# Five loads of raw input weights move from SyncE's queue to ScalarE's, in a channel attention with a SiLU feed-forward layer

## Chip, cores and metric

The kernel runs on one core of one Trainium2 chip. The metric is the device time of one execution in microseconds (us), and the median of several executions is compared.

## What is computed

The reference, cut to what matters: a channel attention over two batches, whose output is the input of a feed-forward layer with SiLU.

```python
def _attn_ref(q, k, v, tau):                       # q, k, v: 2 x 6016 x 256
    qn = q / (np.linalg.norm(q, axis=1, keepdims=True) + 1e-06)
    kn = k / (np.linalg.norm(k, axis=1, keepdims=True) + 1e-06)
    s = kn.transpose(0, 2, 1) @ qn / tau           # 2 x 256 x 256
    a = np.exp(s - s.max(-1, keepdims=True))
    a /= a.sum(-1, keepdims=True) + 1e-09
    return (v @ a).astype(np.float32)

def _moe_ref(x, w_in, w_out):                      # x: 12032 x 256
    h = x @ w_in                                   # 256 x 2048
    g = h * (1.0 / (1.0 + np.exp(-h)))
    return (g @ w_out).astype(np.float32)
```

w_in and w_out come to the chip as 64-bit words, a raw form that the kernel decodes to float.

## The kernel before

The attention matrix of a batch is 256 x 256. So it is computed first and multiplied into w_in; after that the tokens, 1024 at a time, go through a feed-forward layer with the mixed weights. That second part takes some 900 us and is PE's alone. The change lies in the first stage, the first 50 us, which works on batch 0:

- **q and k.** `load_qk` (line 230) brings rows of k and q side by side. The 47 rows j of batch 0 come as four small tiles `g` of one row and then as tiles `kq_t` of two rows (512 KB; the 22nd and last has one row). Seven buffers of pool `st` hold them, so a load waits until the tile seven places back has been read. PE multiplies each tile into the scores `sc` (line 301).
- **Norms.** `attention` squares each tile on ACT (line 296, into `sq`, a tag with two buffers that the squares of v_t use too) and adds the squares up on DVE (line 298, into `acc`, which lies in the space of `wo`). At the end DVE adds the two halves of `acc` (line 292) and the square of the last, half tile. Then PE sums over the partitions: `tot` (line 318), ACT takes the root, DVE the reciprocals `rn` (line 357), and so on to the attention matrix.
- **Raw weights.** `load_wi(j)` (line 1176) loads one of eight blocks of w_in, 512 KB in rows of 2 KB, through `land` (line 172), which issues the DMA. Blocks 0 to 4 go to tiles `raw`, blocks 5 to 7 to the tile `held`. DVE takes the largest value of each (`raw_amax`, line 213, into `raw_max`). Block 0 is decoded early: a CAST on ACT (line 203) and a shift with an OR on DVE (line 205), into `t`.
- **v.** `load_v` brings 1024 tokens of v; `scale_v` squares them on ACT (line 522), takes differences on DVE (lines 585 and 642), and scales and splits them on ACT and DVE (lines 164 and 165).
- **tau** is loaded, spread over the partitions by a matmul `tau_ps` and inverted on DVE.

Each engine works through its instructions in the order in which they stand in the program. That order comes from a scheduling layer, which goes by priorities (the first stage has priority 0, the maxima of the raw blocks a later one) and by its own estimate of when things are ready; only from line 1316 on is the order of PE and DVE written by hand, and later that of ACT. DMAs share eight completion semaphores in turn, so an issue also waits for the DMA eight places back. Issues from SP and from ACT go to two queues. `follow(load, ...)` holds the issues of a load behind the last instruction of SP so far.

The loop of the first stage (line 1234) goes over all tiles, the four small ones first: the score steps of a tile, then `load_qk` for the tile seven places on, and at g = 6, 8, 10, 12 and 14, which are the `kq_t` tiles 3, 5, 7, 9 and 11, a `load_wi` (line 1242).

## Time and profile before

| | us |
|---|---|
| median of three executions | 1007.92 (1007.48 to 1007.94) |
| the profiled execution | 1006.87 |
| its span in the profile | 1005.10 |
| PE busy in the span | 998.5 (99%) |
| DVE, ACT busy | 847.7, 769.5 |
| software queue of GpSimd, SP's queue: moved | 67.98 MB, 68.84 MB |

The span leaves out 1.8 us of the execution around it. PE's clock is granted in full in all forty slices of the page, and its matmuls follow each other nearly without a gap from the first microseconds to the end. The DMA engines are busy for 90% and more of the first tenth of the span, and for a third to a half of the rest. Matmuls of float32 show as two records each: a `kq_t` tile of two rows has eight records on PE.

### The profile page before, as it was taken

Reading aid. Unit: us, or ns where it says so; the run is one execution under the profiler, and the core shown is the slowest. Engines: PE = TensorE matmul, PEld = TensorE weight load, DVE = VectorE, ACT = ScalarE, POOL = GpSimd, SP = SyncE. Lnnn points to the kernel's source line nnn. Section 1 sums busy time; section 2 is a strip of 40 time slices with the busy share of each in tenths; the row PEclk is TensorE's granted clock in tenths of the full one; section 3 lists DMA queues with packets and bytes.
Section 4 is the critical chain, followed back from the end, with each engine's and each line's share of the span. In section 5 each row is a group of like instructions: output and inputs, shape, how many; then the busy total and the mean of one; then the engine's idle time right before and its main releaser. Section 6 shows DMA issues by size and latency. Waiting matters only on the chain.

```text
span 1005.1 us, 20958 instructions
## 1 busy us (share of the span) xinstructions
PE 998.5 (99%) x8554; PEld 869.1 (86%) x8554; DVE 847.7 (84%) x1334; ACT 769.5 (77%) x1081; POOL 199.5 (20%) x283
## 2 busy tenths in 40 slices
PE   9999999999999999999999999999999999999998
PEld 8877555788888888888999988888888888889998
DVE  6997678888888888899889998888888888888776
ACT  6686798788888888878878777677677677677674
POOL 1011000122222222222222212212212212212231
PEclk9999999999999999999999999999999999999999
DMA  9996200546547547526435335335435335335343
GB/s 368 397 397 219 84 1 1 185 103 193 152 135 201 148 129 201 142 72 166 97 74 133 92 91 153 93 95 142 102 95 145 98 95 150 87 96 127 82 99 87
DMA packets 62053, 138.81 MB, mean 138 GB/s; under 512 B 6659, under 2 KB 20915, under 8 KB 61955
## 3 DMA queue, kind: packets, MB, share of 16 engines
q0 software_dynamic: 30672, 67.98, 29.1%
q1 hardware_dynamic: 30850, 68.84, 19.5%
q8 instruction: 67, 1.10, 0.4%
q10 hardware_dynamic: 432, 0.64, 0.2%
q14 instruction: 32, 0.25, 0.1%
HBM read 57.67 MB, written 12.32 MB: 70 GB/s over the span
## 4 chain that ended last, share of the span: by engine, by line
PE 87%; DVE 5%; DMA 4%; ACT 2%; issue 1%; SPq 0%; DVEq 0%; ACTq 0%
PE o L939 38%; PE x L805 21%; PE y L805 10%; PE z L805 5%; PE o L707 4%; DMA kq_t<-in_kq 4%; PE sc L301 3%; PE x L734 2%; PE w L454 2%; DVE g L812 1%; PE y L734 1%; DVE hl L825 1%; ACT hl L822 1%; DVE t L1035 0%; DVE sb L997 0%
## 5 line engine op out<-in xcount | busy, mean ns | idle before, releaser
L805 PEld LDWEIGHTS <-wall 128*128 128x128 f16 x3696 | 360.0, 98 | 37.4 <-issue 1.1
L805 PE MATMUL x<-m,wall 128*128 128x256 f16 (+1 forms) x2112 | 282.9, 270 | 0.5 <-DVE g L812 0.2
L939 PE MATMUL o<-hl,wo 128*128 128x256 f16 (+1 forms) x2136 | 274.1, 270 | 0.0
L825 DVE SCALAR_TENSOR_TENSOR hl<-g,sg,hl 128x1024 f16<-128x1024 f32 (+1 forms) x176 | 221.1, 1257 | 53.4 <-ACT hl L822 52.8
L939 PEld LDWEIGHTS <-wo 128*128 128x128 f16 x2484 | 242.2, 98 | 23.0
L815 ACT ACTIVATE g<-g,alpha 128x512 f32<-128x512 f32 (+3 forms) x176 | 161.5, 921 | 83.0 <-DVE g L812 81.8
L822 ACT ACTIVATE hl<-g,sg 128x1024 f16<-128x1024 f32 (+1 forms) x176 | 198.0, 1126 | 0.0
L1042 POOL DMA_DIRECT2D sums<-hl x109 | 97.3, 892 | 359.0 <-DMA sums<-hl 123.5
L805 PE MATMUL y<-m,wall 128*128 128x256 f16 (+1 forms) x1056 | 141.7, 270 | 0.1
L846 ACT COPY c<-x 128x512 f32<-128x512 f32 (+1 forms) x88 | 50.7, 576 | 74.5 <-PE x L805 74.5
L939 PE MATMUL o<-t,ws_hi 128*128 128x256 f16 (+1 forms) x392 | 93.4, 270 | 0.0
L939 PE MATMUL o<-t,ws_lo 128*128 128x256 f16 (+1 forms) x392 | 93.4, 270 | 0.0
L812 DVE TENSOR_TENSOR g<-x,c 128x512 f32<-128x512 f32 (+1 forms) x88 | 59.5, 677 | 31.2 <-PE x L805 30.9
L815 ACT ACTIVATE g<-x,alpha 128x512 f32<-128x512 f32 (+1 forms) x88 | 58.8, 668 | 26.4 <-PE x L805 25.6
L1035 DVE TENSOR_TENSOR t<-t,hl 128x1024 f16<-128x1024 f16 (+1 forms) x109 | 74.0, 679 | 3.0
L301 PE MATMUL sc<-kq_t 128*128 128x256 f32 x320 | 73.6, 381 | 0.4 <-DMA kq_t<-in_kq 0.4
L812 DVE TENSOR_TENSOR g<-c,y 128x512 f32<-128x512 f32 (+1 forms) x88 | 59.3, 674 | 17.1 <-ACT c L846 14.4
L939 PEld LDWEIGHTS <-ws_hi 128*128 128x128 f16 x696 | 68.1, 98 | 6.5
L939 PEld LDWEIGHTS <-ws_lo 128*128 128x128 f16 x696 | 68.1, 98 | 6.5
L1035 DVE TENSOR_TENSOR t<-hl 128x1024 f16<-128x1024 f16 (+1 forms) x109 | 73.1, 671 | 0.0
L1040 POOL DMA_DIRECT2D sums<-hl x44 | 31.1, 707 | 204.0 <-DVE hl L825 134.5
L805 PE MATMUL z<-m,wall 128*128 128x256 f16 (+1 forms) x528 | 70.7, 270 | 0.0
(193 smaller groups left out, 1343.6 us busy)
## 6 DMA issues: line engine op xcount, KB each, us to landing
sums<-hl POOLq DMA_DIRECT2D x142, 256.0 KB, 3.3
kq_t<-in_kq SPq DMA_DIRECT2D x39, 512.0 KB, 9.0
sums<-t POOLq DMA_DIRECT2D x54, 256.0 KB, 3.0
extra<-hl POOLq DMA_DIRECT2D x42, 256.0 KB, 3.5
v_t<-in_vT SPq DMA_DIRECT2D x10, 1024.0 KB, 5.5
outT<-sb SPq DMA_DIRECT2D x40, 256.0 KB, 3.6
turned<-in_qT SPq DMA_DIRECT2D x10, 512.0 KB, 7.1
turned<-in_kT SPq DMA_DIRECT2D x10, 512.0 KB, 6.2
```

Of the source, the lines that this page charges most:

```text
L301: nc.tensor.matmul(sc[:, cb, :], t[:, i, 0, cb * P : (cb + 1) * P], t[:, i, 1, :], start=(j + i == 0 and cb == 0), stop=(j + i == J - 1), ...
L707: nc.tensor.matmul(o[:, :h], a[:, f, ee], hl[:, m, :h], start=(c == 1 and i == 0), stop=(c == NF and i == 2),)
L805: nc.tensor.matmul(bank[:, k * wide : (k + 1) * wide], mixed[b, i][:, v, a - 1], m[:, c, x, at : at + wide], start=(first and j + k == 0), ...
L812: nc.vector.tensor_tensor(out=g, in0=a[:, :h], in1=c[:, :h], op=ALU.subtract)
L815: nc.scalar.activation(out=g, in_=src, func=AF.Silu, scale=alpha)
L822: nc.scalar.activation(out=hl[:, :, 0], in_=g, func=AF.Copy, scale=sg)
L825: nc.vector.scalar_tensor_tensor(out=hl[:, :, 1], in0=g, scalar=sg, in1=hl[:, :, 0], op0=ALU.mult, op1=ALU.subtract,)
L846: nc.scalar.copy(c2[:, :h], x[:, :h])
L939: nc.tensor.matmul(o[:, side * wide : (side + 1) * wide], a, x, start=(first and j == 0), stop=(last and j == len(these) - 1), skip_group_ ...
L1035: nc.vector.tensor_tensor(out=o, in0=x, in1=y, op=ALU.add)
L1040: nc.gpsimd.dma_start(o, x)
L1042: nc.gpsimd.dma_start(o, y, accum_op=ALU.add)
```

## The change

`load_wi` passes ACT's queue to `land` for blocks 0 to 4, and the first-stage loop ties each of these issues to the last instruction of ACT so far instead of the last of SP. Blocks 5 to 7 stay on SP's queue.

```diff
@@ def load_wi(j):
         if j == 0:
-            raws[j] = land(hp.tile([P, CHUNK + PAD], U16, tag="c51", name="raw"), 0, src)
+            raws[j] = land(hp.tile([P, CHUNK + PAD], U16, tag="c51", name="raw"), 0, src, nc.scalar)
         elif j < 5:
             if j in (1, 3):
                 two[j // 3] = vp.tile([P, 2 * CHUNK + PAD], U16, tag="v", name="raw", bufs=3)
-            raws[j] = land(two[j // 3], (j - 1) % 2, src)
+            raws[j] = land(two[j // 3], (j - 1) % 2, src, nc.scalar)
@@ for g in range(len(groups[0])):
             elif 6 <= g < 16 and g % 2 == 0:
-                follow(load_wi, g // 2 - 3)
+                wait, start = last_of()[mybir.EngineType.Activation], len(traced())
+                load_wi(g // 2 - 3)
+                behind(start, {wait.engine: wait}, {wait.engine})
```

What the scheduling layer makes of it is shown by the order of instructions on each engine, - before and + now. On SP the five issues of raw leave, and the 21 and a half `kq_t` loads stand one behind the other, with v_t and tau between them. On ACT, from the square of the first `kq_t` tile on (`sq` are the squares, `av` the sums of v_t's):

```order
-L296 ACTIVATE sq<-kq_t 128x1024 x6
-L522 ACTIVATE sq,av<-v_t 128x1024
-L296 ACTIVATE sq<-kq_t 128x1024 x2
+L296 ACTIVATE sq<-kq_t 128x1024 x3
+L177 DMA raw<-in_w_in 128x2x1024
+L296 ACTIVATE sq<-kq_t 128x1024
+L203 CAST t<-raw 128x512
+L296 ACTIVATE sq<-kq_t 128x1024
+L177 DMA raw<-in_w_in 128x2x1024
+L296 ACTIVATE sq<-kq_t 128x1024
 L522 ACTIVATE sq,av<-v_t 128x1024
 L296 ACTIVATE sq<-kq_t 128x1024
```

The issue of block 0 now stands behind the square of tile 3, that of block 1 behind the square of tile 5, and in the rows that follow blocks 2, 3 and 4 stand behind those of tiles 7, 9 and 11; the CAST of block 0, which stood behind the square of tile 10, is ahead of that of tile 5.

On DVE, from the addition of the first `kq_t` tile on (`wo` is the space of `acc`):

```order
 L298 TENSOR_TENSOR wo<-wo,sq 128x1024 x4
+L213 TENSOR_REDUCE raw_max<-raw 128x1
 L585 TENSOR_TENSOR x<-v_t 128x512
+L205 SCALAR_TENSOR_TENSOR t<-raw,t 128x512
 L298 TENSOR_TENSOR wo<-wo,sq 128x1024 x2
 L585 TENSOR_TENSOR v_t<-v_t 128x512
+L213 TENSOR_REDUCE raw_max<-raw 128x1
+L298 TENSOR_TENSOR wo<-wo,sq 128x1024
 L642 TENSOR_TENSOR x<-v_t 128x512
```

The maximum of block 0 now stands ahead of the addition of tile 5 and that of block 1 ahead of the addition of tile 7; those of blocks 2, 3 and 4 follow ahead of the additions of tiles 9, 11 and 13. Before, the first stood behind the addition of tile 10.

On DVE again, at the end of the first stage, from the additions of tiles 19 to 21 on:

```order
-L298 TENSOR_TENSOR wo<-wo,sq 128x1024 x3
+L213 TENSOR_REDUCE raw_max<-held 128x1
 L292 TENSOR_TENSOR wo<-wo 128x512
+L213 TENSOR_REDUCE raw_max<-held 128x1
 L298 TENSOR_TENSOR wo<-wo,sq 128x512
-L213 TENSOR_REDUCE raw_max<-held 128x1 x2
 L357 RECIPROCAL rn<-root 128x4
 L358 TENSOR_TENSOR rn<-rn,tot 128x4
```

The maxima of blocks 5 and 6 (`held` 0 and 1) stood behind the last addition and now stand ahead of it. On PE two small matmuls move among the score matmuls: `pb` of v's scale to behind tile 12, and `tau_ps` to behind tile 19 with tau's reciprocal on DVE behind the addition of tile 18. From `tot` on PE's order is unchanged.

## Rows read from the trace of the kernel before

**Rows 1.** The page: busy time of each engine (share of the span) and instructions.

```profile
PE 998.5 (99%) x8554; PEld 869.1 (86%) x8554; DVE 847.7 (84%) x1334; ACT 769.5 (77%) x1081; POOL 199.5 (20%) x283
```

**Rows 2.** Waits of PE, whole span: us in total, times, longest.

```profile
PE sc L301 <- DMA kq_t<-in_kq: 0.4, 2, 0.2
PE w L454 <- ACT wi L164: 0.4, 1, 0.4
PE x L734 <- DVE g L745: 0.3, 1, 0.3
```

**Rows 3.** Busy time by stretch: PE, PEld, DVE, ACT, POOL; clock, DMA share, GB/s.

```profile
15.00:25.00 10.00, 10.00 (x48) 8.81 (x48) 7.73 (x9) 9.10 (x12) 0.00 (x0) 1.00 1.03 404
25.00:35.00 10.00, 10.00 (x47) 8.31 (x46) 9.86 (x18) 7.76 (x10) 0.00 (x0) 1.00 1.04 402
```

**Rows 4.** Timeline of PE: start, us, what, records [idle before, releaser].

```profile
8.01 17.54 PE L301 MATMUL sc<-kq_t 128*128 128x256 f32 x80
25.39 0.22 PE L115 MATMUL pb<-spread,ones 128*128 128x128 bf16 x1
...
46.98 1.03 PE L301 MATMUL sc<-hl 128*128 128x256 f32 x4
47.85 0.95 PE L318 MATMUL tot<-ones,wo 128*128 128x1 f32 x8
```

**Rows 5.** The chain of waits in order of time: start, us, what.

```profile
5.03 9.85 DMA kq_t<-in_kq
...
30.41 10.38 DMA kq_t<-in_kq
40.79 0.04 issue
40.84 6.31 PE sc L301 x28
```

**Rows 6.** Timeline of DVE.

```profile
16.05 2.56 DVE L298 TENSOR_TENSOR wo<-wo,sq 128x1024 f32<-128x1024 f32 x2 [1.73 <-ACT sq L296]
...
46.91 0.69 DVE L298 TENSOR_TENSOR wo<-wo,sq 128x512 f32<-128x512 f32 x1
47.52 0.68 DVE L213 TENSOR_REDUCE raw_max<-held 128x1 f32<-128x512 bf16 x1
48.78 0.69 DVE L213 TENSOR_REDUCE raw_max<-held 128x1 f32<-128x512 bf16 x1 [0.58 <-DMA held<-in_w_in]
49.38 0.17 DVE L357 RECIPROCAL rn<-root 128x4 f32<-128x4 f32 x1
```

**Rows 7.** Timeline of ACT (ACTq is its DMA issue).

```profile
0.74 0.89 ACTq L240 DMA_DIRECT2D g<-in_kq  x2
...
9.85 1.06 ACT L296 ACTIVATE sq<-kq_t 128x1024 f32<-128x1024 f32 x1 [0.23 <-DMA kq_t<-in_kq]
...
14.96 1.06 ACT L296 ACTIVATE sq<-kq_t 128x1024 f32<-128x1024 f32 x1 [2.77 <-DMA kq_t<-in_kq]
...
24.38 0.76 ACT L203 CAST t<-raw 128x512 f16<-128x512 bf16 x1
...
48.83 0.26 ACT L329 ACTIVATE root<-tot,tiny 128x4 f32<-128x4 f32 x1 [1.00 <-PE tot L318]
```

**Rows 8.** DVE from 16 to 47.6 us by line: busy, mean ns | idle before.

```profile
L298 DVE TENSOR_TENSOR wo<-wo,sq 128x1024 f32<-128x1024 f32 (+1 forms) x18 | 21.5, 1192 | 3.9 <-ACT sq L296 3.0
```

**Rows 9.** DMA issues from 0.7 to 6 us: count, KB each, us to landing.

```profile
g<-in_kq ACTq DMA_DIRECT2D x2, 256.0 KB, 4.3
```

**Rows 10.** DMA queues from 70.5 to 73.5 us (q1 SP, q0 GpSimd): packets, MB, share.

```profile
q1 hardware_dynamic: 181, 0.67, 57.0%
q0 software_dynamic: 144, 0.52, 45.3%
```

**Rows 11.** The tile raw in the first 75 us.

```profile
DMA to landing us min/median/max: 8.8/10.5/10.9
```

## Prediction

> **What bounds the kernel now.** I read the page first: PE is busy for 998.5 of 1005.1 us [rows 1], so the span is PE's work plus the few moments when PE has nothing to do. The waits of PE name them: tenths of a microsecond each [rows 2]. The change touches the first 50 us only, and after that PE's instructions stand in an unchanged order, so the forecast is how much later (or earlier) PE gets through the first stage.

> There three things are nearly full at once. The DMA engines are at share 1.03 to 1.04, some 400 GB/s, and DVE is busy for 7.73 us and then 9.86 us of ten [rows 3]. PE needs 17.38 us for its first ten kq_t tiles (80 records from 8.01 to 25.39 [rows 4]), 1.73 us a tile; a tile of 512 KB takes 0.524 MB / 0.404 = 1.3 us of all DMA engines. So kq_t alone gives PE 0.43 us of slack a tile, and each raw load of the same size eats 1.3 us. I number the kq_t tiles 1 to 22 (22 is a half one). The chain of waits shows where PE hangs on a landing: tile 5 lands at 5.03 + 9.85 = 14.88, tile 19 at 30.41 + 10.38 = 40.79, and PE runs from 40.84 [rows 5] to the hl matmuls at 46.98 and tot at 47.85 [rows 4]. From 8.01 to 46.98 PE has 21.5 x 1.73 = 37.2 us of tiles and 0.45 of others, so it waits for about 1.3 us in all. The last of DVE's additions (0.69 us from 46.91, [rows 6]) is done at 47.60, just ahead of tot, which reads it.

> **What moves.** On SP's queue raws 0 to 4 stood behind tiles 10, 12, 14, 16 and 18. On ACT they stand behind the squares of tiles 3, 5, 7, 9 and 11: seven tiles earlier. No byte is saved: all that had landed ahead of tile 19 still lands ahead of it, at the same rate, so tile 19 stays at 40.79, but the tiles before it come later. Four prices follow.

> *Issue time.* An ACT issue takes 0.89 / 2 = 0.45 us [rows 7]; five take 2.2. ACT idles for 2.77 us ahead of tile 5 [rows 7] and is busy for 9.10 of the ten us from 15 [rows 3], so some of it shows, but through DVE's waits, counted below. SP loses five issues that waited for nobody PE needs: nothing gained.

> *PE's own path.* If all five raws are ahead of tile n, n lands at 40.79 - 1.3 x (19 - n), and PE then has (22 - n) x 1.73 + 0.87 + 0.2 left. For n = 19 that is 47.0, as measured. Raw 4 is issued behind the square of tile 11, at about 29, and lands at about 33.4, which is ahead of tile 14: 34.3 + 13.8 + 1.1 = 49.2. For n = 16 it is 36.9 + 10.4 + 1.1 = 48.4. With 0.87 us of hl matmuls tot cannot start before 49.3 to 50.1, by 1.4 to 2.2 us later than now.

> *The two reduces that pass the last addition.* Before, the raw_max of held 0 and 1 stood behind the last addition; now they stand ahead of it. Held 1 lands at 48.78, where DVE sat idle for it [rows 6]. The bytes ahead of it are the same, so I keep 48.78: + 0.60 for its reduce (DVE's pace: 47.52 + 0.68 less overlap) + 0.61 for the half addition = 49.99. **This is a floor** for tot of 50.05, or +2.2 us, whatever the rest does.

> *DVE's queue.* In the 31.55 us from 16.05 to 47.60 DVE idled for 3.9 - 1.73 = 2.2 us (the 1.73 lies ahead of 16.05) [rows 6, 8], so its work is 29.35 us. After the change it has 0.6 more (a subtraction that was done by then) and 1.2 more (the two held reduces): 31.2. It starts when raw 0 has landed, since raw 0's reduce is now ahead of the addition of tile 5. Raw 0 is issued at 10.95, as the square of tile 3 ends [rows 7]. How long a raw takes on ACT's queue beside a full SP queue no row shows. The nearest: the two 256 KB g loads took 4.3 us on ACT's queue [rows 9], and where two queues were at work over 3 us each got about half (0.67 and 0.52 MB, [rows 10]). Half the rate makes 512 KB last 2.6 us; adding the 4.3 - 1.3 = 3.0 us that g had beside its bytes gives 5.6; but part of those 3.0 is the start of the whole program, and with 1.3 alone it would be 3. On SP's queue a raw takes 10.5 [rows 11], behind the loads that stand there. I take 4.4 and keep 3.0 and 5.6. Raw 0 then lands at 15.3, tile 5 at 14.88 + 1.3 = 16.2, and the CAST of raw 0, now ahead of tile 5's square on ACT instead of at 24.38 [rows 7], hides under that. 15.3 + 31.2 = 46.5 without a wait. The waits that the new order brings: raw 1 is issued behind the square of tile 5 (17.2), lands at 21.6, and DVE is there at 20.5: 1.05. The second square of v_t waits for the addition behind that reduce (23.4), tile 9's square ends at 25.6, raw 3 is issued there, shares with raw 2 and lands at 30.2, while DVE is there at 28.8: 1.4. Additions that wait for a square or a scale on ACT: 1.3 together. The end is at 50.3. The reciprocal of tau has moved to behind the addition of tile 18 and needs a PE matmul that now stands behind tile 19 (PE is there at about 45.0, DVE at 44.15): up to 0.85, so 50.3 to 51.2. I take 51.0 for tot, **+3.15 us** on 47.85.

> What comes back: the reduce of held 1 held up the first reciprocal behind tot (49.38, while the root was there at 48.83 + 0.26 = 49.09) [rows 6, 7]; it is done earlier now, so 0.25 us. Behind that nothing on PE moved; its later waits of 0.4 and 0.3 us [rows 2] are for ACT and DVE work that starts from tot and shifts with it. Part of that work is in another order on DVE and ACT: 0 taken, -0.7 to +0.7 kept. Sum: 3.15 - 0.25 = +2.9. The profiled run had 1006.87 us, 1.05 below the median of 1007.92; its forecast is 1009.8, that against the median **1010.8**.

> **Rivals.**
> *Far slower.* If a raw takes 5.6 us, each turn of the ring gets longer: square, issue, landing, reduce, addition, next square (two sq buffers). Raw 0 then lands at 16.5, raw 1 at 23.8, raw 3 at 33.6, raw 4 at 37.4; DVE's remaining 16 us behind raw 4's reduce (nine additions, three L165, two reduces, the rest) end at 53.8: +5.95 - 0.25 = 5.7, so 1013.6. It decides from 5 us on. For it: raw rows are of 2 KB against 4 KB for kq_t, and if the DMA engines alternate row by row a raw gets a third of the time, not half. Against: in [rows 10] both queues get about equal bytes.
> [...]

> *Level.* Raws land in 3 to 4 us, PE is not late by itself, and only the floor is left: 50.05 - 47.85 - 0.25 = +1.95, 1009.9; with held 1 landing a little earlier or a later wait gone, down to 1008.9. For it: DVE still had 2.2 us of idle time.

> *Faster.* SP's queue carries kq_t alone and the 1.3 us that PE waits for its tiles go: 1006.6. It decides if the raws only take up DMA time that PE does not need, that is if they come after the tiles have run ahead. Against: PE has no slack at all at tile 5 (14.88 against 14.9), raw 0 goes right ahead of it, and the floor on held 1 would have to fall too.

> **How the numbers follow.** Forecast 0.55 (1010 to 1011.7), far slower 0.20, level 0.17, faster 0.08. The range of 1009.0 to 1014.0 leaves out the faster case, the lower part of the level one and the end of the far slower one. A measurement here tells 0.2%, 2.0 us, from no change: slower 0.75 (the forecast and the far slower case), the same 0.19 (level, and a small part of faster), faster 0.06.

> **What would show it.** Right: tot's first matmul near 51, PE idle ahead of it behind DVE's last addition; DVE idle ahead of the reduces of raw 1 and raw 3; tile 5's matmuls at 16.2; held 1 landing near 48.8; CAST of raw 0 at 15 to 16. The later waits unchanged. Wrong: tot at 48 to 49 (held 1 landed early, or the additions were not what tot waited for), raws landing after 6 us, or PE's time lost somewhere behind 55 us.

## Result and profile after

The changed kernel takes 1018.84 us (median of four executions, 1017.25 to 1019.45) against 1007.92 before: ratio 1.011, 95% interval 1.0098 to 1.0122, that is +10.9 us. The forecast was 1010.8 (range 1009.0 to 1014.0). The direction and the place were right, and the forecast had about a quarter of the size. The profiled execution of after took 1019.05 us with a span of 1017.3, 12.2 more than the span of before.

The busy times answer to [rows 1]: PE has 5.2 us more busy time for the same 8554 instructions, about half of it in the stretch behind `tot` that is shown below; DVE, ACT and GpSimd have what they had.

```profile
PE 1003.7 (99%) x8554; PEld 873.0 (86%) x8554; DVE 847.4 (83%) x1334; ACT 769.9 (76%) x1081; POOL 199.9 (20%) x283
```

The timeline of PE in the first stage, columns as in [rows 4] (`sc<-hl` are the first scores of batch 1, `rq_ps` spreads the reciprocals that are made from tot):

```profile
32.81 0.26 PE L115 MATMUL pb<-spread,ones 128*128 128x128 bf16 x1 [2.64 <-DVE spread L110]
...
51.39 1.03 PE L301 MATMUL sc<-hl 128*128 128x256 f32 x4
57.24 1.84 PE L318 MATMUL tot<-ones,wo 128*128 128x1 f32 x8 [4.82 <-DVE wo L298]
...
62.50 1.01 PE L376 MATMUL rq_ps<-diag,ones 128*128 128x128 f32 x4
```

tot starts at 57.24 instead of 47.85 [rows 4]: 9.4 us later, and PE stood idle for the last 4.8 of them behind DVE's last addition. From tot to rq_ps it is then 5.26 us, where before it was 2.75 (47.85 to 50.60 in the trace of before). These 2.5 us are PE's clock: with it at 1.00 in a run below, tot to rq_ps takes 2.67. Here the stretches (columns of [rows 3]) show it granted at 0.50 behind the idle wait:

```profile
57.00:59.00 2.00, 1.76 (x9) 1.79 (x9) 0.10 (x1) 0.00 (x0) 0.00 (x0) 0.50 1.05 402
59.00:62.50 3.50, 3.50 (x10) 2.78 (x10) 1.88 (x8) 1.75 (x3) 0.00 (x0) 0.50 1.03 407
```

So the loss is 9.4 ahead of tot, 2.5 behind it and 0.3 in the rest. Why tot is late stands in the chain of waits (start, us, what), the view of [rows 5]. There, before, the DMAs on the chain were loads of kq_t and, at the start, of g; now three of five raw loads are on it:

```profile
9.76 7.96 DMA raw<-in_w_in
...
17.80 0.05 ACT t L203
...
17.90 9.28 DMA raw<-in_w_in
27.21 0.04 DVE raw_max L213
...
27.81 1.23 DVE wo L298
...
30.24 1.07 ACT sq L296
31.33 1.24 DVE wo L298
32.60 8.23 DMA raw<-in_w_in
40.85 0.03 DVE raw_max L213
```

From raw 1's landing on, this is the ring that the far-slower rival describes: a landing, the reduce on DVE, the addition behind it, a square on ACT that needs the freed buffer, the next issue behind that square. From raw 0 to raw 1 the link is shorter: the issue of raw 1 stands behind the CAST of raw 0 on ACT (L203), which waits for the same landing. The three landings take 25.5 of the first 41 us. So in time the loads moved forward little: on SP's queue they were issued at 13.80, 17.46, 20.82, 25.14 and 29.06 us, on ACT's at 9.76, 17.90, 22.00, 30.25 and 32.60. Only the first is earlier. What moved are the readers: the five reduces, at 26.14 to 41.15 us before, are now at 17.74 to 40.85, four of them directly behind the landing that DVE waited for.

The same on DVE, to be read against [rows 6] and [rows 8]: from 13 us on every break of DVE is a raw that has not landed, and from 41 us to the last addition there is none.

```profile
17.74 0.69 DVE L213 TENSOR_REDUCE raw_max<-raw 128x1 f32<-128x512 bf16 x1 [4.26 <-DMA raw<-in_w_in]
...
27.21 0.69 DVE L213 TENSOR_REDUCE raw_max<-raw 128x1 f32<-128x512 bf16 x1 [4.49 <-DMA raw<-in_w_in]
...
34.77 0.69 DVE L213 TENSOR_REDUCE raw_max<-raw 128x1 f32<-128x512 bf16 x1 [0.88 <-DMA raw<-in_w_in]
...
40.85 0.69 DVE L213 TENSOR_REDUCE raw_max<-raw 128x1 f32<-128x512 bf16 x1 [2.41 <-DMA raw<-in_w_in]
...
56.41 0.68 DVE L298 TENSOR_TENSOR wo<-wo,sq 128x512 f32<-128x512 f32 x1
```

On ACT (as [rows 7]) an issue takes 0.37 to 0.39 us and does not wait for the end of the square ahead of it: four start within 0.02 us of that square's start, and that of raw 1 while the CAST runs, 0.54 us before its square. It costs ACT nothing: the squares with an issue at their start take 1.06 us, as those without. What costs is the CAST of raw 0, which stands ahead of the square of tile 5 and waits, and the square of v_t behind DVE's wait for raw 1:

```profile
9.74 1.06 ACT L296 ACTIVATE sq<-kq_t 128x1024 f32<-128x1024 f32 x1 [0.22 <-DMA kq_t<-in_kq]
9.76 0.39 ACTq L177 DMA_DIRECT2D raw<-in_w_in  x1
...
17.80 0.78 ACT L203 CAST t<-raw 128x512 f16<-128x512 bf16 x1 [5.71 <-DMA raw<-in_w_in]
17.90 0.39 ACTq L177 DMA_DIRECT2D raw<-in_w_in  x1
18.44 1.99 ACT L296 ACTIVATE sq<-kq_t 128x1024 f32<-128x1024 f32 x2
...
29.06 1.06 ACT L522 ACTIVATE sq<-v_t 128x1024 f32<-128x1024 f32 x1 [5.06 <-DVE wo L298]
```

What a landing is made of can be read from the DMA queues (packets, MB, share, as [rows 10]; q1 is SP's, q10 ACT's) in two stretches, the first just behind the issue of raw 0 and the second while it moves. In 9.7 to 13.2 us:

```profile
q1 hardware_dynamic: 380, 1.43, 102.1%
```

and in 13.4 to 17.2 us:

```profile
q1 hardware_dynamic: 279, 1.01, 67.0%
q10 hardware_dynamic: 268, 0.52, 36.8%
```

From the issue at 9.76 us on, not a byte of raw moves for 3.6 us. Then the two queues move about equally many rows (253 of 2 KB and 247 of 4 KB; the other packets have 4 bytes), and since raw's have 2 KB and those of kq_t 4 KB, raw gets a third of the bytes (0.52 of 1.53 MB) and needs 3.6 us for its 512 KB (its rows start from 13.35 to 16.99). From issue to landing, to be read against [rows 11], the tile raw has

```profile
DMA to landing us min/median/max: 4.5/8.0/9.3
```

In the order of issue the five took 8.0, 9.3, 7.1, 4.5 and 8.2 us. The 4.5 is raw 3, issued at 30.25. SP's queue still had all of the DMA engines for the 2.1 us to its first row (101.3% of their time), but then little to move (0.16 MB in 1.8 us), and all of raw 3's rows started within 1.9. SP's queue was short of work because SP's issues wait too; of SP's waits in the first 60 us (us in total, times, longest) this is the largest, where in before it was 1.2:

```profile
SPq L240 <- DMA raw<-in_w_in: 11.6, 3, 7.3
```

These are loads of kq_t that stand eight DMAs behind a raw and share its completion semaphore: the three waits end at 17.73, 27.20 and 29.12 us, and raws 0, 1 and 2 landed at 17.72, 27.18 and 29.11.

### The profile page after: what moved, and what is told of

It reads as the page before. It is cut to its first block, busy times and chain, and to the rows that moved or that the text cites. A ratio compares the mean times of both kernels' runs of the same rounds, so it can differ in the third digit from the quotient of the medians.

```text
span 1017.3 us, 20960 instructions
## 1 busy us (share of the span) xinstructions
PE 1003.7 (99%) x8554; PEld 873.0 (86%) x8554; DVE 847.4 (83%) x1334; ACT 769.9 (76%) x1081; POOL 199.9 (20%) x283
## 3 DMA queue, kind: packets, MB, share of 16 engines
q0 software_dynamic: 30672, 67.98, 28.8%
## 4 chain that ended last, share of the span: by engine, by line
PE 86%; DVE 6%; DMA 4%; ACT 2%; issue 1%; SPq 0%; DVEq 0%; ACTq 0%
PE o L939 37%; PE x L805 21%; PE y L805 10%; PE z L805 5%; PE o L707 4%; PE sc L301 3%; DMA raw<-in_w_in 3%; PE x L734 2%; PE w L454 2%; DVE wo L298 1%; PE y L734 1%; DVE g L812 1%; DMA kq_t<-in_kq 1%; ACT hl L822 1%; DVE hl L825 1%
## 5 line engine op out<-in xcount | busy, mean ns | idle before, releaser
L301 PEld LDWEIGHTS sc<-kq_t 128*128 128x128 f32 x320 | 61.0, 194 | 14.0 <-issue 2.9
L1040 POOL DMA_DIRECT2D sums<-hl x44 | 31.2, 709 | 203.5 <-DVE hl L825 134.9
```

The costliest lines, as they stand in the source:

```text
L301: nc.tensor.matmul(sc[:, cb, :], t[:, i, 0, cb * P : (cb + 1) * P], t[:, i, 1, :], start=(j + i == 0 and cb == 0), stop=(j + i == J - 1), ...
L1040: nc.gpsimd.dma_start(o, x)
```

## Experiments

The theory from the two traces: the loads are on the path because their readers on DVE and ACT stand closer behind the issue than the 8 us that a landing takes. Its rivals: the other queue costs by itself (its issues, its rows, the completions that both queues share), or the early bytes do, since they come ahead of tiles that PE needs. Each experiment ran beside the kernel before on the same chip, in three groups, in which before had 1007.48, 1007.32 and 1007.39 us; differences (+) are against these. The expectations count the experiments in the order in which they ran: their first is the other queue without the order of the readers, their second the issues later, their fourth the 80 extra matmuls, their fifth the bytes four tiles earlier.

### The order of the readers without the other queue

The kernel before, its loads on SP's queue, with the reduces where the change has them (the diff is against before; each reduce is held behind the addition ahead of it, and the next addition behind the reduce):

```diff
+            if 8 <= g < 18 and g % 2 == 0:
+                start = len(traced())
+                raw_amax(raw_max[:, j : j + 1], raws[j])
+                behind(start, adds[g - 1], {mybir.EngineType.DVE})
+                reduced = {mybir.EngineType.DVE: traced()[-1]}
...
+            if reduced:
+                behind(start, reduced, {mybir.EngineType.DVE})
...
-    with at(RAW):
-        for j in range(5):
-            raw_amax(raw_max[:, j : j + 1], raws[j])
```

> The kernel before, with all loads on SP's queue at their old places; only the five reduces are put where the change has them on DVE: ahead of the additions of tiles 5, 7, 9, 11 and 13 (the CAST stays late). Theory A: DVE stands at the reduce of block 0 until that load has landed at 22.7 instead of 17.7, the additions, squares and buffers behind it follow, tot at 58 or later, total 1018 to 1026. Theory B: within 2 us of the kernel before, 1008 to 1010.

Measured: 1019.17 us (1018.55 to 1020.35), ratio 1.0118 (1.0103 to 1.0133), +11.7 us, as slow as the change itself. PE's row of tot:

```profile
57.43 1.84 PE L318 MATMUL tot<-ones,wo 128*128 128x1 f32 x8 [6.75 <-DVE wo L298]
```

DVE waits 10.1 us for raw in two waits, the longer one 8.4. So readers that stand ahead of their data suffice for a loss of this size, and ACT's queue is not needed for it. That the size is the same is partly chance: on SP's queue raw 0 lands at 22.67 us instead of 17.72, DVE's waits are two instead of four, and the scheduling layer puts the reduces of held 0 and 1 ahead of the last addition here too.

### The other queue without the order of the readers

The change, with the reduces of raw, the decode of raw 0 and the reduces of held 0 and 1 held behind the additions behind which they stood before:

```diff
             raw_amax(raw_max[:, j : j + 1], raws[j])
+            behind(start, adds[13 + 2 * j], {mybir.EngineType.DVE})
...
         spend(decoded[0], 3)
+        behind(start, adds[13], {mybir.EngineType.DVE, mybir.EngineType.Activation})
...
             raw_amax(raw_max[:, j : j + 1], raws[j])
+            behind(start, adds[25], {mybir.EngineType.DVE})
```

> The five loads stay on ScalarE's queue behind the same squares; only their readers go back: the five reduces stand on DVE behind the additions of tiles 10, 12, 14, 16 and 18, the two of held behind the last addition, and block 0 is decoded behind tile 10. Theory A (the loss of 11 us is DVE and ACT standing in order behind loads that land 7 to 9 us after their issue): no engine waits for raw any more, tot starts at 48 to 50 instead of 57.2, total 1008 to 1010.5. Theory B (the second queue itself: its loads take DMA time from kq_t, and SP's issues wait for their semaphores): tot stays at 55 or later, total 1015 to 1019.

Measured: 1011.13 us (1009.79 to 1011.46), ratio 1.0034 (1.0020 to 1.0048). No reduce waits for raw any more, tot starts at 51.45, and in the profiled execution (1010.36 us) PE's clock stays full and tot to rq_ps takes 2.69 us. Two thirds of the loss are gone. What is left, +3.7 us, is more than the early bytes were expected to cost; later experiments split it.

### The issues later, the readers as the scheduling layer puts them

```diff
-            elif 6 <= g < 16 and g % 2 == 0:
+            elif 13 <= g < 22 and g % 2 == 1:
...
-                load_wi(g // 2 - 3)
+                load_wi((g - 13) // 2)
```

> The five loads stay on ScalarE's queue but are issued behind the squares of tiles 10, 12, 14, 16 and 18, seven tiles later than in the change; the scheduler puts the reduces two or three tiles behind each issue. Theory A: the reduces stand 4 to 5 us behind the issue again and the loads land after 6 to 8, so DVE waits again, tot at 51 to 55, total 1011 to 1016. Theory C (it is the early place of the loads, which pushes kq_t back): with the late place total 1007.5 to 1009.5.

Measured: 1015.28 us (1014.7 to 1015.9), ratio 1.0078 (1.0063 to 1.0093), +7.8 us. PE is through with its tiles in time (the first hl matmuls at 46.23, before 46.98), and still tot waits 6.21 us, to 53.46: DVE waits 5.6 us for raw. The place of the bytes is no cure as long as the readers move with the loads.

### More distance between issue and reader

The change, with each issue behind the square of the tile of its own step, two tiles earlier, and the reduces held in their places as in the first experiment above:

```diff
-            elif 6 <= g < 16 and g % 2 == 0:
-                wait, start = last_of()[mybir.EngineType.Activation], len(traced())
-                load_wi(g // 2 - 3)
+            if 4 <= g < 14 and g % 2 == 0:
+                wait, start = adds[g][mybir.EngineType.Activation], len(traced())
+                load_wi(g // 2 - 2)
```

> The five loads stay on ScalarE's queue, but each is issued two tiles earlier (behind the squares of tiles 1, 3, 5, 7 and 9), while the reduces stay ahead of the additions of tiles 5, 7, 9, 11 and 13 as in the changed kernel. Only the distance from issue to reader grows, by two turns of some 2 us each. Theory A (the loss is the landing, 8 us after the issue, less what lies between issue and reader): VectorE's waits for raw fall from 12.0 us to 3 to 6, tot starts at 51 to 54, and the sum is 1010 to 1014.5 us. Rival B (the bytes ahead of tiles 4 to 12 and the shared DMA engines are the loss, whatever the distance): the tiles come still earlier into want, tot at 56 or later, 1016 us or more.

Measured: 1010.58 us (1010.25 to 1011.03), ratio 1.003 (1.0020 to 1.0040), +3.2 us: 7.7 us of the loss come back by issuing two tiles earlier, where the early bytes, were they the price, would have cost more. About 2.5 of the 7.7 are the clock, which stays full here (tot to rq_ps takes 2.70 us). DVE's wait for raw (us in total, times, longest):

```profile
DVE raw_max L213 <- DMA raw<-in_w_in: 4.3, 3, 2.2
```

And PE's row of tot:

```profile
51.67 1.02 PE L318 MATMUL tot<-ones,wo 128*128 128x1 f32 x8 [0.76 <-DVE wo L298]
```

The landings are no shorter here (7.9 to 9.6 us); they lie further ahead of their readers.

### Rows of 4 KB

```diff
-            flat[:, at + 1 : at + 1 + CHUNK].rearrange("p (k n) -> p k n", k=k),
+            flat[:, at + 1 : at + 1 + CHUNK].rearrange("p (k n) -> p k n", k=src.shape[1]),
...
+        if j < 5:
+            src = wi_src[:, j // 4 : j // 4 + 1, j % 4 * 2 * C : (j % 4 + 1) * 2 * C]
```

> The changed kernel, but each of the five loads brings one row of 4 KB for each partition instead of two of 2 KB (the same bytes; it takes another part of w_in, so the weights that come out are not those of the reference). Theory A (the two queues alternate row by row, so rows of 2 KB beside rows of 4 KB get about a third): with equal rows a raw's bytes take some 2.6 us instead of 3.5 to 4, each landing comes about 1 us earlier, VectorE's waits for raw fall from 12.0 to 8 to 10 us, tot starts at 53.5 to 56, 1015 to 1017.5 us. Rival B (the landing is mostly the wait before the first byte, or the share goes by something other than rows): landings within 0.5 us of those of the changed kernel, 1018 to 1019.5 us.

Measured: 1015.04 us (1014.37 to 1015.78), ratio 1.0072 (1.0055 to 1.0090), +7.7 us, 3.3 less than the change, at the far end of theory A. The landings of the tile raw:

```profile
DMA to landing us min/median/max: 6.5/6.8/7.5
```

The queues in 13.2 to 16.4 us:

```profile
q1 hardware_dynamic: 195, 0.73, 58.7%
q10 hardware_dynamic: 144, 0.52, 43.4%
```

The rows of raw 0 start within 2.5 us instead of 3.6, but the first of them as late as in the change, 3.5 us behind the issue, and so it is for each of the five here (3.0 to 3.6 for four of the change's, 2.1 for raw 3). DVE's wait for raw falls from 12.0 to 8.0 us, tot starts at 53.35. So the landing of raw 0 was 3.5 us of start, where it had 3.6 with rows of 2 KB, then 2.5 of bytes instead of 3.6, then 0.8 from the start of the last row to the landing (0.5 to 1.7 in the change).

### The reduces of held behind the last addition

```diff
         for j in (5, 6):
             raw_amax(raw_max[:, j : j + 1], raws[j])
+            behind(start, summed, {mybir.EngineType.DVE})
```

> The changed kernel with one part undone: the reduces of held 0 and held 1 stand behind the last addition again, as before the change. VectorE is busy without a break from 41 us to the last addition at 56.4, so these two reduces cost it 1.2 us of work ahead of tot. Theory A (they are 1.2 us of the loss, and the raw landings the rest): tot at 55.7 to 56.4, 1017 to 1018.2 us. Rival B (the floor of the prediction: held 1's landing bounds the end): more than 2 us less, below 1016.5 us.

Measured: 1017.46 us (1016.79 to 1018.2), ratio 1.0098 (1.0077 to 1.0119), +10.1 us, 0.9 less than the change; the executions of the two overlap, so the 0.9 alone is not clear of the noise. In the profiles DVE's last addition starts at 55.66 instead of 56.41 and tot at 56.50 instead of 57.24. These two reduces cost 0.7 to 0.9 us, less than their own 1.2; the sum is theory A's, and the landing of held 1 bounds nothing.

### PE kept busy through its wait

The change with extra matmuls ahead of tot, 80 and then 116:

```diff
-            tot = small_psum("tot")[:, : 2 * KC]
+            tot = small_psum("tot")
+            for _ in range(80):
+                nc.tensor.matmul(tot[:, 256 : 256 + P], ones16, ones16, start=True, stop=True)
+            tot = tot[:, : 2 * KC]
```

> The changed kernel with 80 small bf16 matmuls on constants ahead of tot, in a part of its PSUM tile that nobody reads; they take some 4.5 us and fill most of PE's wait of 4.8 us. Theory D (the half clock granted from 57 to 62.5 comes from PE's idle time ahead of it, and costs 2.5 us between tot and rq_ps): tot starts at 57.2 as in the change, rq_ps 2.75 us later instead of 5.26, total 1016 to 1016.7. If the clock falls for another reason: 1018 to 1020 as in the change.

> The changed kernel with 116 extra matmuls of constants (bf16, 128x128) ahead of tot, whose result nobody reads: about 6.7 us of work for PE in the stretch in which it waited 4.8 us for the last addition. In the fourth experiment 80 of them (4.6 us) left PE idle for 2.15 us, and tot to rq_ps took 3.7 us instead of 5.26. Theory A (the 2.5 us that tot to rq_ps takes longer in the changed kernel come from PE's clock, granted at half after the idle wait): clock 1.00 from 51 to 62 us, tot within 0.3 us of 57.2, tot to rq_ps 2.7 to 3.0 us, 1016.0 to 1016.8 us. Rival B (the later path is longer for another reason): 1017.3 to 1019 us.

Measured: 1017.40 us (1017.29 to 1018.53) with 80 extra matmuls and 1017.10 (1016.62 to 1017.46) with 116, ratios 1.0101 and 1.0096 (1.0081 to 1.0111 for the second). With 116, PE's row of tot, and then the same two stretches as in the profile after:

```profile
59.13 1.00 PE L321 MATMUL tot<-ones,wo 128*128 128x1 f32 x8
```

And the stretches:

```profile
57.00:59.00 2.00, 2.00 (x40) 2.00 (x37) 0.50 (x1) 0.00 (x0) 0.00 (x0) 1.00 1.06 407
59.00:62.50 3.50, 3.50 (x28) 3.19 (x26) 1.82 (x9) 1.75 (x3) 0.00 (x0) 1.00 1.03 408
```

The clock stays full there and tot to rq_ps takes 2.67 us, so the 2.5 us behind tot are the clock. With 80, PE still waits 2.15 us ahead of tot, the clock is at 0.50 from 59.1 to 62.5 us (the mean of the profiled execution is 0.998, and rq_ps takes 1.06 us instead of 0.61 with 116), and tot to rq_ps takes 3.66. The total gives back only 1.1 (+9.8 us), since the extra matmuls ran on past DVE's last addition and tot itself starts 1.9 later; the figure of theory A, 1016.0 to 1016.8, left that out.

### The bytes four tiles earlier, on SP's queue

The kernel before, its readers held where they stood, with the loads behind those of tiles 6, 8, 10, 12 and 14 (the first one in the loop of the first loads):

```diff
+            if g == 9:
+                follow(load_wi, 0)
...
-            elif 6 <= g < 16 and g % 2 == 0:
-                follow(load_wi, g // 2 - 3)
+            if 4 <= g < 12 and g % 2 == 0:
+                follow(load_wi, g // 2 - 1)
```

> The kernel before with the five raw loads on SyncE's queue four tiles earlier (behind the loads of tiles 6, 8, 10, 12 and 14); the reduces and the CAST of raw 0 stay where they were among the additions. It has the early bytes of the changed kernel and of the first experiment, without ScalarE's queue and without early readers. Theory A (what is left in the first experiment, +3.65 us over before, is the early bytes: tiles 7 to 18 land later, PE runs out of them): 1009.5 to 1011.5 us, PE waits 1 us or more in all for tiles kq_t, tot starts at 49.5 to 51.5. Rival B (it is ScalarE's queue and the completion semaphores that both queues share): 1007.0 to 1008.5 us, tot within 0.7 us of 47.85.

Measured: 1008.81 us (1008.24 to 1009.24), ratio 1.0015 (1.0005 to 1.0024), +1.5 us. PE's row of tot:

```profile
49.75 0.95 PE L318 MATMUL tot<-ones,wo 128*128 128x1 f32 x8
```

It is 1.9 us later than before, PE does not wait ahead of it, and nothing but PE's own tiles sets it. The sum lies between the two theories: early bytes cost 1.5 us here, and the queue with its readers in the old order has 2.2 more.

### The small matmuls back in their old place

The queue with its readers in the old order, and tau_ps (first pair of lines) and pb (the steps of v) emitted earlier, with the scores of tile 11 held behind pb:

```diff
-            if g == 22:
+            if g == 13:
                 tau_ps = small_psum("tau_ps")[:, :1]
...
-            if g == 15:
+            if g == 13:
+                next(vgen)
                 next(vgen)
...
+            if g == 14:
+                behind(start, {small.engine: small}, {small.engine})
```

> The first experiment (loads on ScalarE's queue, their readers in the old order, 1011.1 us), and in addition the small matmuls pb and tau_ps back behind tile 10 on TensorE, as before the change, instead of behind tiles 12 and 19. The early bytes alone cost 1.5 us (fifth experiment, 1008.8 us). Theory A (what is left, 2.3 us, is VectorE's waits for pb and tau_ps, 1.7 and 0.7 us in the first experiment, since the scheduling layer moved them): 1008.3 to 1009.6 us. Rival B (it is SyncE's waits for completions that both queues share, 11.1 us there): 1010.3 to 1011.5 us, with SyncE still waiting for raw and VectorE's last addition late at 50 us or more.

Measured: 1009.68 us (1009.1 to 1012.05), ratio 1.0022 (1.0013 to 1.0032), +2.3 us: between the theories, with 1.4 of the 2.2 us gone. In part that seems to be the clock again: of the five executions with pb and tau_ps late, three had a mean clock of 0.998 and took 1011.1 to 1011.5 us, two had 1.000 and took 1009.8 and 1010.4; here PE waits 0.8 us ahead of tot instead of 1.3. The other 0.8 us are left, and SP still waits 11.5 us for raw. Whether they are SP's waits or something else in the queue is open: no run here changes the sharing of completions alone.

### The issues late and the readers later still

The late issues on ACT's queue, with each reduce some five additions behind its load, the decode of raw 0 behind the addition of tile 15 and the reduces of held behind the last one (the diff below leaves these two out):

```diff
-            elif 6 <= g < 16 and g % 2 == 0:
+            elif 13 <= g < 22 and g % 2 == 1:
...
-                load_wi(g // 2 - 3)
+                load_wi((g - 13) // 2)
...
             raw_amax(raw_max[:, j : j + 1], raws[j])
+            behind(start, adds[min(18 + 2 * j, 24)], {mybir.EngineType.DVE})
```

> The loads go by ScalarE's queue, but behind the squares of tiles 10, 12, 14, 16 and 18, and each reduce stands some five additions behind its load (held's behind the last addition, the decode of raw 0 behind the addition of tile 15), so that nobody should stand behind a landing. Theory A (the queue itself costs PE nothing if no engine waits for its loads and the bytes come late): 1007.0 to 1009.0 us, no wait of VectorE for raw over 0.5 us, tot at 47.3 to 49. Rival B (the shared completion semaphores hold up SyncE's issues of kq_t and held all the same, as SyncE waited 11.1 us for raw landings in the first experiment and 9.1 in the second): 1010 to 1012 us, with waits of PE for kq_t of over 1 us, or held 1 late.

Measured: 1010.72 us (1008.13 to 1012.01), ratio 1.003 (1.0016 to 1.0044), +3.4 us, inconclusive on the queue. No reduce waits for raw, but four of them now fall among DVE's last additions, DVE waits 1.94 us for the late tau_ps, and tot waits 2.42 us for DVE in the profiled execution (1008.13 us, mean clock 1.0). The executions of 1010.7 us and above had a mean clock of 0.996: there a drop of the clock probably came on top.

### The bytes four tiles later, on SP's queue

The kernel before, with the loads behind those of tiles 14, 16, 18, 20 and 22:

```diff
-            elif 6 <= g < 16 and g % 2 == 0:
+            elif 10 <= g < 20 and g % 2 == 0:
-                follow(load_wi, g // 2 - 3)
+                follow(load_wi, g // 2 - 5)
```

> The kernel before with the five raw loads on SyncE's queue four tiles later (behind the loads of tiles 14, 16, 18, 20 and 22), that is a move of the same bytes to the other side. If the place of the bytes sets PE's waits in the first stage (theory A): PE loses less of its 1.3 us there, and the sum is 1006.5 to 1008 us. Rival: VectorE has the reduces of five raw blocks left behind the last additions, or held 0 and 1 land later, ahead of rn: tot within 0.5 us of 47.85, rn 1 to 4 us later, 1008.5 to 1012 us.

Measured: median 1006.36 us (1005.91 to 1010.43), ratio 0.9996 (0.9986 to 1.0005). PE no longer waits for tiles (the first hl matmuls at 46.03), and tot starts at 47.60. The median is 1.0 us lower, which theory A had, but one of ten executions was 3 us above before (1010.43; one of the 18 of before in another group had 1010.61), and the interval includes no change: no version here is shown to beat the kernel before.

## Why the prediction was wrong

**The failed step: the landing of a raw.** The prediction put 4.4 us, with bounds of 3.0 and 5.6; it was 8.0 (median), 8.0, 9.3 and 8.2 for the three on the chain. Both halves were too small. The start was worked out, as at most 3.0 us, from the two g loads, which were issued at 0.74 us when the DMA engines had nothing to do [rows 9]; their first row came 1.3 us behind the issue, and beside a full SP queue it was 3.0 to 3.6. The lower bound of 3.0 for a landing does not come out of its own terms, as 2.6 and 1.3 make 3.9. The bytes were taken at half the rate from [rows 10], where both queues had rows of like size; with rows of 2 KB beside rows of 4 KB they got a third (0.52 of 1.53 MB). The row that was nearer in the state that matters, full DMA engines, was [rows 11] with 10.5 us, and the prediction set it aside because a raw stands behind other loads there. With 8 to 9 us in the prediction's ring the end of DVE moves to where it was seen: DVE waits 4.49 us at raw 1 (1.05 predicted), 0.88 at raw 3 (1.4) and 2.41 at raw 4 (none), raw 4 landed at 40.8, and the 16 us that the far-slower rival put behind it were 16.3 (40.85 to 57.1). Two smaller steps failed with it: the CAST of raw 0, which was to hide under the landing of tile 5, kept ACT waiting for 5.71 us and held up the issue of raw 1; and raw 4, taken as issued at about 29 us, was issued at 32.60, since the ring slows its own issues.

**Right: the ring and DVE's work.** DVE's 31.2 us of work were 31.0 (busy time from 16.05 to 57.10), the wait at raw 1 and the square of v_t behind it are where they were put, and the order alone on SP's queue gives a loss of the same size. The far-slower rival had the mechanism, rows that alternate, and fell short by 5 us: 2.5 of them are the clock, and its 5.6 us of landing were too few.

**Wrong: the row weighed against that rival.** The prediction had the equal bytes of [rows 10] against it, but there both queues had rows of like size. In the change 253 rows of the one queue moved beside 247 of the other in the same 3.8 us, and with equal rows the landing was 6.8 us instead of 8.0 (medians): both fit sharing row by row. So do the times of the single rows. The trace names no engine for a row, but where just one row starts 4 ns ahead of another's end, which is the most frequent step, it is of the other queue in 211 of 224 cases from 13.4 to 16.9 us. The trace of before held this too: 95 of 97 from 2.7 to 3.5 us, where g loads of 2 KB rows ran on both queues.

**Right: PE's own path.** Predicted was tot at 49.3 to 50.1 without DVE; with early bytes alone, on SP's queue, it was at 49.75. In the change itself PE also waited 2.64 us for pb and ran at half clock behind that, and reached the hl matmuls at 51.39.

**Right, but smaller: issue time.** 2.2 us were allowed for as partly hidden; ACT loses nothing, and raw 0 was issued at 9.76 us, as its square started, instead of 10.95, as it ended.

**Wrong: the floor on held 1 and the rate behind it.** The step said that the same bytes ahead mean the same landing at 48.78. It needs DMA engines that are always full. With SP's issues held up, 45 to 50 us had 293 GB/s, where before it was 387. But DVE came to the reduces of held at 54.6 and found them landed, so the floor bound nothing; the two reduces cost 0.7 to 0.9 us. The same premise left out that SP's issues would wait for raws, 11.6 us in all.

**Missing: the clock.** No term had PE's clock in it. PE idled for 4.8 us, and the next 5.26 us were granted half (0.50 from 56.5 to 63.3 us). Of the 0.25 us that should come back at rn, 0.1 came where the clock stayed full (2.67 instead of 2.75 us from tot to rq_ps with 116 extra matmuls); in the change rn waits 2.32 us for the root.

**The sum again**, in the profiled executions: DVE's waits from 16.05 us to its last addition went from 2.3 us to 10.0, its work there from 29.3 to 31.0, together 9.5, and tot is 9.4 later; the clock adds 2.5, the rest 0.3: 12.2 us. The medians differ by 10.9, since the profiled execution of before was 1.05 below its median and that of after 0.2 above.

## What to carry to other kernels

Moving the loads to another queue saved no transfer time here; it moved the issues, and the scheduling layer moved the readers along. Before such a move, set the distance from issue to the first reader against a landing time that was measured with the DMA engines as full as they will be, not one from an idle stretch, and ask which engine stands behind that reader in program order. Where the reader is not urgent, pin it late: with the readers in their old places the same loads cost a third here.
